# Threshold attention with an MLP: the threshold sums moved from VectorE to ScalarE, and the first loads split evenly over two queues, keys first

## The chip, the cores and the metric

The kernel runs on one core of a Trainium2 chip. The metric is the device time of one execution in microseconds (us), the median of the runs. Kernels are compared through the ratio to the unchanged kernel, run in turn with them on the same chip.

## The reference

Eight batches of eight heads with 576 tokens and head size 64, then an MLP with a squared ReLU over all 4608 tokens:

```python
scores = scale * np.matmul(q, k.transpose(0, 1, 3, 2))
thresh = np.max(scores, axis=-1, keepdims=True) - tau
scores = np.where(scores >= thresh, scores, -1000000000.0)
scores = scores - np.max(scores, axis=-1, keepdims=True)
attn = np.exp(scores)
attn = attn / (np.sum(attn, axis=-1, keepdims=True) + 1e-09)
attn_out = np.matmul(attn, v)
# heads side by side: x is (4608, 512)
h = x @ w_in            # 512 x 2048
r = np.maximum(h, 0.0)
out = (r * r) @ w_out   # 2048 x 512
```

## The kernel before

A *visit* handles a pair of heads, a *step* one block of 128 queries of both heads. Each step computes scores into PSUM, takes the row maxima on VectorE, adds -8 tau to get the threshold, exponentiates on ScalarE, and then masks and sums in one VectorE pass, after which the PSUM is free for the next scores. `s` is the PSUM tile of the scores (single buffered, one per head), `st` a small SBUF tile with a column per scalar.

```python
def scores(s):
    ...                                            # matmuls into sc[u]      (L199)
    mx, thr = (st[:, j, 0:n] for j in range(2))
    for u in range(n):
        nc.vector.tensor_reduce(out=mx[:, u:u + 1], in_=sc[u][:, :, 0:HALF], axis=AX.XY, op=ALU.max)   # L204
    nc.vector.tensor_scalar(out=thr, in0=mx, scalar1=ntau8, scalar2=None, op0=ALU.add)                 # L205

def exponents(vis, i):
    nc.scalar.activation(out=bias, in_=mx, func=AF.Copy, scale=-SCALE)                                 # L213
    for u in range(len(sc)):
        nc.scalar.activation(out=w..., in_=sc[u]..., func=AF.Exp, bias=bias[:, u:u + 1], scale=SCALE)  # L215

def threshold(vis, i):
    for u in range(n):                                                                                 # L227
        nc.vector.scalar_tensor_tensor(out=wu, in0=sc[u]..., scalar=thr[:, u:u + 1], in1=wu,
                                       op0=ALU.is_ge, op1=ALU.mult, accum_out=sm[:, u:u + 1])
    nc.vector.tensor_scalar(out=den, in0=sm, scalar1=S * LITTLE, scalar2=None, op0=ALU.max)            # L229
    nc.vector.reciprocal(rcp, den)

def prep(n):                                       # 32x32 blocks of queries and keys turned on VectorE (L178)
    for to, rows in zip((qT, kT), rows_of(n)):
        nc.vector.transpose(to, rows.rearrange("p c d -> p (c d)"))
```

In the order of VectorE's queue, L204 and L205 of a step are followed either by `prep` of the next visit (two transposes), or by three instructions that round a piece of the MLP's weights (L137, L138, L140), or by neither; then comes L227. GpSimd divides (L239), squares (L378) and does the last two steps of the rounding (L142, L144). TensorE runs one fixed queue: scores (L199), transposes of the weights of attention (L257), mixing with v (L318), and pieces of the MLP (L367 and the products L398, L430) spread between.

## Time and profile before

| | before |
|---|---|
| median of the runs ahead of the prediction | 1455.95 us |
| span of the profiled execution | 1448.2 us |
| TensorE, VectorE, ScalarE, GpSimd busy | 96, 62, 29, 43% |
| first score matmul | 8.97 us |
| threshold sums L205 on VectorE, busy | 57.4 us in 160 |

The lines that the argument rests on are in the prediction. One more of the page is of use later: the matmul clock that was granted, in tenths, in 40 slices of 36 us each. A trace's clock records know full and half speed only; the halved stretches are 3.4 or 6.8 us long here, so a slice that shows 8 held several us of half clock. The records don't start with the program: the first one of this trace is at 25.8 us, and what comes before it is counted as full speed.

```profile
PEclk9899999999999999999999999999999999999999
```

### The profile page before, as it was taken

The page shows a single profiled execution, that of the slowest core. Times are in us where ns is not written, and L with a number is a line of the kernel's source. Part 1 is how long each engine was busy: PE and PEld are TensorE (multiplying, and loading weights), DVE is VectorE, ACT ScalarE, POOL GpSimd, SP SyncE. Part 2 cuts the span into 40 slices and gives each one's busy share as a digit, 9 for nine tenths or more (in the row PEclk, how much of TensorE's full clock was granted, in tenths as well). Part 3 has the DMA queues.
Part 4 walks back from the last instruction along what each step waited for, and adds up shares of the span by engine and source line. Part 5 has one row for each costly group of instructions (what it writes and reads, how often), then busy time and mean ns, then how long its engine had stood idle before and what let it go on. Part 6 is the DMA issues. An engine that isn't in the chain of part 4 may idle for free.

```text
span 1448.2 us, 22131 instructions
## 1 busy us (share of the span) xinstructions
PE 1387.1 (96%) x7412; PEld 1058.0 (73%) x7412; DVE 904.5 (62%) x1930; ACT 423.1 (29%) x904; POOL 623.9 (43%) x794
## 2 busy tenths in 40 slices
PE   5898888999999999999999999999999999999998
PEld 3676555747787777777777777777777777788887
DVE  5899886568766676666675767666667666631011
ACT  3666554223222322222322222222222222210100
POOL 3588765425343444343343435343434352422321
PEclk9899999999999999999999999999999999999999
DMA  7564442345445545545455454555554445440000
GB/s 149 119 140 109 112 112 52 55 84 96 85 96 91 109 85 96 88 92 88 97 96 105 84 96 85 95 89 100 95 101 84 89 90 91 90 81 19 5 15 15
DMA packets 532528, 125.94 MB, mean 87 GB/s; under 512 B 523712, under 2 KB 523712, under 8 KB 532416
## 3 DMA queue, kind: packets, MB, share of 16 engines
q1 hardware_dynamic: 529984, 124.24, 44.7%
q8 instruction: 60, 0.98, 0.3%
q10 hardware_dynamic: 2400, 0.30, 0.2%
q14 instruction: 52, 0.43, 0.1%
q0 software_dynamic: 32, 0.00, 0.0%
HBM read 48.63 MB, written 9.44 MB: 40 GB/s over the span
## 4 chain that ended last, share of the span: by engine, by line
PE 65%; SPq 20%; DVE 6%; issue 3%; DMA 2%; ACT 2%; POOL 1%; DVEq 0%; ACTq 0%; POOLq 0%
PE bank L367 26%; PE bank L430 16%; SPq L299 12%; PE s L199 9%; PE bank L318 8%; SPq L306 5%; PE bank L398 3%; SPq L161 3%; DVE st L204 2%; PE bank L257 1%; SPq L163 1%; DVE w L227 1%; DVE turned L288 1%; DMA vs<-in_v_dram 1%; DVE turned L138 1%
## 5 line engine op out<-in xcount | busy, mean ns | idle before, releaser
L367 PE MATMUL bank<-xT,w_in_sb 128*128 128x256 f32 x2304 | 519.8, 382 | 3.5 <-POOL w_in_sb L144 2.4
L367 PEld LDWEIGHTS bank<-xT,w_in_sb 128*128 128x128 f32 x2304 | 431.6, 190 | 84.2 <-issue 21.3
L204 DVE TENSOR_REDUCE st<-s 128x1 f32<-128x576 f32 x288 | 206.7, 753 | 296.9 <-PE s L199 296.9
L378 POOL TENSOR_TENSOR g<-g 128x512 f32<-128x512 f32 x144 | 149.8, 1042 | 232.2 <-ACT g L377 209.4
L239 POOL TENSOR_SCALAR w<-w,st 128x576 f32<-128x576 f32 x269 | 236.4, 888 | 31.2 <-DVE st L230 25.2
L227 DVE SCALAR_TENSOR_TENSOR w<-s,st,w 128x576 f32<-128x576 f32 x269 | 207.3, 803 | 52.2 <-ACT w L215 51.9
L430 PE MATMUL bank<-wo,gsum 128*128 128x256 f32 x1024 | 234.2, 382 | 2.9 <-DVE u_sum L445 1.6
L430 PEld LDWEIGHTS bank<-wo,gsum 128*128 128x128 f32 x1024 | 192.5, 190 | 38.6 <-issue 7.6
L199 PE MATMUL s<-kT,qT 64*128 64x288 f32 x1024 | 176.8, 438 | 30.4 <-DVE kT L178 10.3
L237 POOL TENSOR_SCALAR st<-st 128x2 f32<-128x2 f32 (+1 forms) x160 | 38.7, 242 | 379.7 <-DVE w L227 366.1
L215 ACT ACTIVATE w<-s,st 128x576 f32<-128x576 f32 x269 | 186.1, 738 | 12.1 <-ACT st L213 0.4
L318 PE MATMUL bank<-wT,vs 128*64 128x128 f32 (+3 forms) x1700 | 179.7, 358 | 8.7 <-DMA wT<-turned 3.5
L430 PE MATMUL bank<-wo,g 128*128 128x256 f32 x768 | 178.7, 383 | 2.9 <-DVE osb L449 2.9
L199 PEld LDWEIGHTS s<-kT,qT 64*128 64x128 f32 x1024 | 101.1, 190 | 95.2 <-issue 71.4
L288 DVE STREAM_TRANSPOSE turned<-w 128x576 f32<-128x576 f32 x225 | 163.0, 758 | 10.1 <-DMA wT<-turned 3.8
L430 PEld LDWEIGHTS bank<-wo,g 128*128 128x128 f32 x768 | 143.8, 190 | 32.4 <-issue 8.2
L318 PEld LDWEIGHTS bank<-wT,vs 128*64 128x64 f32 x1700 | 107.9, 141 | 78.1 <-issue 25.6
L377 ACT ACTIVATE g<-bank 128x512 f32<-128x512 f32 x144 | 86.3, 599 | 200.7 <-PE bank L367 200.7
L213 ACT ACTIVATE st<-st 128x2 f32<-128x2 f32 (+1 forms) x160 | 33.2, 208 | 328.2 <-DVE st L204 327.5
L332 ACT COPY xT<-bank 128x256 f32<-128x256 f32 x42 | 15.7, 373 | 287.9 <-PE bank L318 287.9
L443 DVE TENSOR_TENSOR gsum<-g 128x512 f32<-128x512 f32 x32 | 20.8, 681 | 107.3 <-PE bank L430 107.3
L398 PE MATMUL bank<-wo,g 128*128 128x512 f32 x128 | 62.0, 619 | 7.3 <-POOL wo L144 7.0
(66 smaller groups left out, 858.1 us busy)
## 6 DMA issues: line engine op xcount, KB each, us to landing
wT<-turned SPq DMA_DIRECT2D x800, 72.0 KB, 2.2
ql<-in_q_dram SPq DMA_DIRECT2D x128, 72.0 KB, 2.5
vs<-in_v_dram SPq DMA_DIRECT2D x72, 128.0 KB, 2.5
wo<-in_moe_w_in_dram SPq DMA_DIRECT2D x16, 512.0 KB, 4.5
wo<-in_moe_w_out_dram SPq DMA_DIRECT2D x16, 512.0 KB, 3.6
out_dram<-osb SPq DMA_DIRECT2D x32, 256.0 KB, 2.3
kl<-in_k_dram SPq DMA_DIRECT2D x62, 72.0 KB, 2.6
wT<-turned SPq DMA_DIRECT2D x200, 20.0 KB, 1.9
```

The lines of the kernel that those rows point to most:

```text
L199: nc.tensor.matmul(sc[u][:, half, 0:HALF], lhsT, kT[rows, half * HALF:(half + 1) * HALF], start=True, stop=True)
L204: nc.vector.tensor_reduce(out=mx[:, u:u + 1], in_=sc[u][:, :, 0:HALF], axis=AX.XY, op=ALU.max)
L215: nc.scalar.activation(out=w[:, u, :].rearrange("p (h k) -> p h k", h=2), in_=sc[u][:, :, 0:HALF], func=AF.Exp, bias=bias[:, u:u + 1], sca ...
L227: nc.vector.scalar_tensor_tensor(out=wu, in0=sc[u][:, :, 0:HALF], scalar=thr[:, u:u + 1], in1=wu, op0=ALU.is_ge, op1=ALU.mult, accum_out=s ...
L239: nc.gpsimd.tensor_scalar(out=w[:, u, :], in0=w[:, u, :], scalar1=z[:, u:u + 1], scalar2=rcp[:, u:u + 1], op0=ALU.add, op1=ALU.mult)
L288: nc.vector.transpose(wb[:, u * KB:(u + 1) * KB, i % 2, :], w[:, u, :].rearrange("p (k q) -> p k q", q=32))
L299: nc.sync.dma_start(out=to[:, :, at:at + 64], in_=wb[rows, j::4, :, :].rearrange("p c u q -> p c (u q)"))
L318: nc.tensor.matmul(ps[u * D:(u + 1) * D, 0:nq], vs[n % 2][:, u * (NBLK + 1) + c, :], wT[:, cw, cols], start=(c == 0), stop=(c == NBLK))
L367: nc.tensor.matmul(h[:, x % 2, :], w_in_sb[:, c, f * P:(f + 1) * P], xT[:, c, at:at + TCH], start=(c == 0), stop=(c == NMC - 1))
L378: nc.gpsimd.tensor_tensor(out=to, in0=to, in1=to, op=ALU.mult)
L398: nc.tensor.matmul(o[t].rearrange("p (h d) -> p h d", h=2), g[:, f, t * P:(t + 1) * P], mov, start=(f == 0), stop=(f == NFT - 1))
L430: nc.tensor.matmul(to, left[:, f, :], wo[:, slot, f, :], start=(f == 0), stop=(f == HF - 1))
```

## The change

It is meant to shorten VectorE's queue and to have the first visit's data in SBUF sooner.

```diff
 def load_qk(n):
-        for x, t in zip(rows_of(n), (q, k)):
-            queue = nc.scalar if n == 0 and t is k else nc.sync
+        for x, t in list(zip(rows_of(n), (q, k)))[::-1]:
             for m in range(4):
+                queue = nc.scalar if n == 0 and m % 2 else nc.sync
 def scores(s):
-        mx, thr = (st[:, j, 0:n] for j in range(2))
+        mx = st[:, 0, 0:n]
         ...
-        nc.vector.tensor_scalar(out=thr, in0=mx, scalar1=ntau8, scalar2=None, op0=ALU.add)
 def exponents(vis, i):
-        mx, bias = (st[:, j, 0:len(sc)] for j in (0, 2))
+        mx, thr, bias = (st[:, j, 0:len(sc)] for j in range(3))
         nc.scalar.activation(out=bias, in_=mx, func=AF.Copy, scale=-SCALE)
+        nc.scalar.activation(out=thr, in_=mx, func=AF.Identity, bias=ntau8)
```

## The prediction

> **What bounds the kernel now.** I read the busy shares first, then a table of six stretches of time, then the matmul engine's waits, then the rows of the instructions that the change touches, and last the timeline of single steps. (A "step" is one block of 128 queries of one pair of heads.) The busy shares:
>
> ```profile
> PE 1387.1 (96%) x7412; PEld 1058.0 (73%) x7412; DVE 904.5 (62%) x1930; ACT 423.1 (29%) x904; POOL 623.9 (43%) x794
> ```
>
> TensorE is the bound over the whole, VectorE is at 62% and ScalarE at 29%, so the change moves work from a half loaded engine to a lightly loaded one, and neither is the bound. Whether there is a gain depends on the stage. Columns: stretch, its length, then busy us (number of instructions) of PE, PEld, DVE, ACT, POOL, then clock, DMA share and GB/s:
>
> ```profile
> 0.00:9.00 9.00, 0.03 (x2) 0.04 (x2) 1.71 (x3) 1.28 (x1) 2.83 (x10) 1.00 0.87 109
> 9.00:82.00 73.00, 56.80 (x369) 41.59 (x370) 59.34 (x131) 40.64 (x89) 35.21 (x48) 0.88 0.61 132
> 82.00:250.00 168.00, 149.14 (x1073) 99.40 (x1074) 142.58 (x292) 99.03 (x220) 124.52 (x139) 0.98 0.43 106
> 250.00:300.00 50.00, 50.00 (x273) 34.78 (x268) 26.76 (x59) 15.39 (x33) 18.97 (x27) 1.00 0.36 65
> 300.00:1320.00 1020.00, 1006.49 (x5123) 774.30 (x5122) 658.11 (x1416) 256.02 (x542) 415.67 (x547) 1.00 0.50 91
> 1320.00:1448.20 128.20, 124.59 (x584) 107.92 (x582) 15.98 (x32) 10.78 (x20) 26.71 (x24) 1.00 0.03 13
> ```
>
> From 250 us to the end TensorE is busy 1181.1 of 1198.2 us: 17 us idle, in which nothing on VectorE or ScalarE can save more than a few. Before 250 us it is busy 206.0 of 250: 9 us of first loads, 16 us idle between 9 and 82, 19 us idle between 82 and 250. As TensorE runs its queue in a fixed order and is dense later, a microsecond saved here comes off the end. The waits of TensorE say on what:
>
> ```profile
> PE s L199 <- DVE w L227: 11.8, 9, 3.5
> PE s L199 <- DVE kT L178: 10.3, 4, 9.0
> PE s L199 <- DVE wo L227: 9.7, 5, 3.3
> PE bank L398 <- POOL wo L144: 7.0, 5, 2.6
> ```
>
> The scores (L199) wait 21.5 us in 14 steps for the threshold pass L227, which frees their PSUM, and once 9.0 us for the first transposed keys. So the early chain is: scores, row maximum L204, threshold sum L205, other VectorE work of the step, L227, next scores. The change takes L205 out of it.
>
> **What the Trainium skill says.** (1) "SBUF — State Buffer", section "Who interferes with whom": a VectorE tensor_scalar may enter a two-port mode, and then it and GpSimd exclude each other for a whole instruction. The trace agrees: L205 on 128x2 lasts 228 ns in the median but 1327 at most, and here it ends with a GpSimd instruction:
>
> ```profile
> 55.39 1.31 DVE L205 TENSOR_SCALAR st<-st,ntau 128x2 f32<-128x2 f32 x1
> 55.40 1.27 POOL L144 TENSOR_TENSOR w_in_sb<-turned 128x512 f32<-128x512 f32 x1
> 55.82 0.22 ACT L213 ACTIVATE st<-st 128x2 f32<-128x2 f32 x1
> 56.13 1.37 ACT L215 ACTIVATE wo<-s,st 128x576 f32<-128x576 f32 x2
> 56.61 0.77 DVE L178 STREAM_TRANSPOSE qT<-ql 128x576 f32<-128x576 f32 x1
> 57.31 0.73 DVE L178 STREAM_TRANSPOSE kT<-kl 128x576 f32<-128x576 f32 x1
> 57.97 0.77 DVE L227 SCALAR_TENSOR_TENSOR wo<-s,st,wo 128x576 f32<-128x576 f32 x1
> ```
>
> (2) "ScalarE: Activation LUTs", section "What ACT_TABLE_LOAD costs": an ACTIVATE with immediate operands costs 186 ns plus 0.833 ns an element, each pointer operand adds about 93, back-to-back ones overlap by about 93; cheap functions such as Identity are in every table set. The trace has 208 ns for L213, the immediate form on two elements, against 188 by the page. (3) "DMA: Bandwidth & Descriptors", section "Issuing engines are not separate DMA queues": two issuing queues share the same engines and save only issue time. The trace shows those engines 87% busy in the first 9 us. (4) "TensorE: Matmul & The Clock Gate", Part 1, says idle windows of about 3.4 us halve the matmul clock. Here the eight score matmuls take 3.00 us at 14.73 and 21.03 us and 1.24 at 632.40: agreed.
>
> **The change, part by part.** The rows:
>
> ```profile
> L205 DVE TENSOR_SCALAR st<-st,ntau 128x2 f32<-128x2 f32 x128 | 50.6, 396 | 4.5
> L205 DVE TENSOR_SCALAR st<-st,ntau 128x1 f32<-128x1 f32 x32 | 6.8, 214 | 1.1
> L213 ACT ACTIVATE st<-st 128x2 f32<-128x2 f32 x128 | 26.6, 208 | 239.6 <-DVE st L204 238.9
> ```
>
> Removed from VectorE: 50.6 + 6.8 = 57.4 us of busy time. Only 160 x about 0.22 = 35 us of it is work; some 22 us is waiting for GpSimd. As instructions overlap, a free L205 really pushes the next instruction back by 0.13 to 0.2 us (12 steps of the timeline read this way).
>
> Added on ScalarE: 160 x (208 + 93 = 301 ns, estimate from the row and the page) = 48 us of busy time, ScalarE to about 471 us or 32%. It stands between the bias and the exponentials. The exponential now starts about 0.04 us after the bias ends; with the threshold between and the overlap, I estimate 0.15 to 0.2 us later. No second table load appears in the compiled program.
>
> So in each early step either VectorE gates L227 (gain) or the exponential does (loss of about 0.2). Going through the twelve steps up to 82 us: step 0 is gated by ScalarE (VectorE sat idle 0.78 us before L227): -0.15. Step 1, transposes between: +0.18. Step 2, ScalarE gates: -0.2. Step 3: VectorE and ScalarE ready together, and TensorE goes on late for other reasons: 0. Step 4: +0.13. Step 5 (L205 blocked for 1.31 us before the transposes): L227 can come 0.37 earlier, then ScalarE gates, and TensorE has other work until 0.2 us before: +0.2. Step 6: +0.05. Step 7, the one shown above: transposes can start at 55.4, and end at 56.8; the exponential would end near 57.05; L227 moves from 57.97 to 57.05, and TensorE sat idle 1.81 us for it: +0.9. Step 8: 0, TensorE-bound. Step 9: L205 waited 0.2 for GpSimd, but the next instruction (L137, weight rounding, also a tensor_scalar) will wait in its place: +0.1. Steps 10 and 11: +0.13 and +0.1. Sum: 1.44 us.
>
> 82 to 250 us: 24 steps, of which TensorE's waits show only a few gated by L227; there the blocked L205 is mostly followed by weight rounding, which inherits the wait. The rounded weights come a little sooner to L398. I put 0.8 us (about 6 steps of 0.13). After 250 us: 0.1.
>
> First loads: ten DMAs for the first visit, before as four on one queue and six on the other, now five and five. The compiled listing shows that the DMAs rotate over eight semaphores, so that the ninth and tenth wait for early ones to land; in the trace these were key loads issued at 3.97 and 4.95 us, and the last key landed at 8.13. Now the two late ones are query loads, on both queues at about 4.0: landing near 7.2. But VectorE still transposes queries first (7.03 to 7.8 before, while the keys were coming in) and keys second. Now both transposes must follow the last landing: 7.2 + 1.5 = 8.7 against 8.13 + 0.78 = 8.91. Gain 0.15 to 0.2, not 0.9: loading keys first works against the order of the transposes. I take 0.15.
>
> Sum: 0.15 + 1.44 + 0.8 + 0.1 = 2.5 us.
>
> **Rivals.** (a) ScalarE becomes the gate: L227 waits 51.9 us in 44 places for the exponential already. If the addition costs its full 0.3 us in every gated early step, and the gains do not show, about +3 us: 1459. Against it: ScalarE is 29% busy, and past 250 us TensorE has other matmuls to run meanwhile. (b) The clock: if step 7 shrinks, TensorE's idle gap before the scores at 58.90 halves, and these (2.69 us, warm 1.24) and the mixing matmuls after them (2.40 us, warm 1.31) may run warm. That would add 1 to 2 us to the gain: 1451.5. I count 0.6 for it. (c) The wait just moves: GpSimd excludes the next tensor_scalar instead of L205 everywhere, and the gain is the first loads and steps 5 and 7 only: 1454.7. (d) The first loads turn out worse, if one late query load lands at 8 us: start at 9.5, +0.6 us. The second visit's keys and queries come in swapped order too, but are needed only at 18.7 us.
>
> **Range and chances.** 1455.95 - 2.5 - 0.6 = 1452.8 us. The three runs before spread over 2.7 us, so a noise of 1.3 either way; with the rivals 1448.5 to 1456.8. Two per cent would be 29 us, more than all of TensorE's idle time between 9 and 82 us: faster 0.01, same 0.98, slower 0.01.
>
> **What would show it.** First score matmul at 8.6 to 8.9 us instead of 8.97. TensorE waiting under 1.2 us instead of 1.81 for the L227 of step 7. VectorE busy down by 35 to 57 us, or less where L137 and L138 inherit blocking: their means (437 and 880 ns) would rise. A new ScalarE row near 0.3 us a piece, its busy time up 40 to 50. PE idle before 82 us down by 1 to 3 us, and PE from 300 us on unchanged. I am wrong if the exponential's wait on the early steps grows so that TensorE idles longer before 82 us, if the matmul total after 300 us changes by more than 3 us, or if the first scores start after 9.2.

## The result, and the profile after

| | before | after |
|---|---|---|
| median, same chip, four runs each | 1456.62 us | 1444.49 us |
| ratio, 95% interval | | 0.9916 [0.9899, 0.9933] |
| once more on another chip, 11 and 6 runs | 1452.02 us | 1439.97 us, ratio 0.9926 [0.9911, 0.9942] |

A ratio is the mean time of one kernel's runs over that of the other's of the same rounds, so not quite the ratio of the medians. The change saves 11 to 12 us (0.0084 x 1456.6 = 12.2, and 0.0074 x 1452.0 = 10.7). The prediction said 1452.8 us and 1448.5 to 1456.8: within 2%, as forecast, but outside the range, and the gain more than three times the 3.1 us foretold (2.5 for the change and 0.6 for the clock).

The busy shares after, to be held against those of before: VectorE lost 50.4 us of busy time, ScalarE gained 12.6.

```profile
PE 1384.3 (96%) x7412; PEld 1057.4 (73%) x7412; DVE 854.1 (59%) x1770; ACT 435.7 (30%) x1064; POOL 620.9 (43%) x794
...
PEclk9999999999999999999999999999999999999999
```

ScalarE's small rise surprises only until one looks at the group itself. The sums take 36.6 + 9.0 = 45.6 us, but they overlap the bias ahead of them and the exponential after them, and busy time counts overlapping time once. The rows of the new instruction (it is L213 of the changed kernel; the bias, L213 before, has become L212) and of two others that stayed on VectorE (busy us, mean ns, then the idle time before them):

```profile
L213 ACT ACTIVATE st<-st,ntau 128x2 f32<-128x2 f32 x128 | 36.6, 286 | 0.0
...
L213 ACT ACTIVATE st<-st,ntau 128x1 f32<-128x1 f32 x32 | 9.0, 282 | 0.0
```
```profile
L137 DVE TENSOR_SCALAR turned<-wo 128x512 uint32<-128x512 uint32 x32 | 19.4, 605 | 0.0
...
L229 DVE TENSOR_SCALAR st<-st 128x2 f32<-128x2 f32 x128 | 38.8, 303 | 4.4
```

L137 had a mean of 437 ns before and L229 265: part of the blocking by GpSimd that L205 suffered was handed to the next tensor_scalar, as predicted. It is 5.4 us at L137 (19.4 against 14.0) and 4.8 at L229 (38.8 against 34.0), some 10 of the 22 us.

Now the step that the prediction shows (step 7), in the timeline after. Columns: start, duration, engine, line, operation.

```profile
52.86 0.77 DVE L178 STREAM_TRANSPOSE qT<-ql 128x576 f32<-128x576 f32 x1
52.98 1.28 POOL L144 TENSOR_TENSOR w_in_sb<-turned 128x512 f32<-128x512 f32 x1
...
53.51 0.29 ACT L213 ACTIVATE st<-st,ntau 128x2 f32<-128x2 f32 x1
53.55 0.73 DVE L178 STREAM_TRANSPOSE kT<-kl 128x576 f32<-128x576 f32 x1
...
54.49 0.82 DVE L227 SCALAR_TENSOR_TENSOR wo<-s,st,wo 128x576 f32<-128x576 f32 x1 [0.21 <-ACT wo L215]
...
55.47 0.72 PE L199 MATMUL s<-kT,qT 64*128 64x288 f32 x2 [0.80 <-DVE wo L227]
```

The same GpSimd instruction runs, but no VectorE instruction stands behind it: the transposes go on beside it. TensorE waits 0.80 us where it waited 1.81, and L227 now waits a little for the exponential. That much is the mechanism of the prediction. What does not fit is the size, and one thing more: the stretch of 9 to 82 us shows TensorE *busy* for as long as before.

```profile
9.00:82.00 73.00, 57.38 (x405) 41.71 (x403) 60.58 (x128) 44.06 (x108) 40.43 (x53) 1.00 0.68 144
300.00:1320.00 1020.00, 1006.64 (x5133) 777.17 (x5132) 616.59 (x1295) 265.69 (x658) 411.86 (x544) 1.00 0.50 91
```

Before it was 56.80 us there, for 369 matmuls; now 57.38 us, for 405. A window of fixed ends hides a gain that shifts work into it. The Trainium skill, "Trainium Kernel Development and Optimization", section "Performance Expectations", calls matmul busy time a bad metric for how close a kernel is to its limit, because matmuls are pipelined. It is no measure of progress in these traces either: nearly equal busy time, a tenth more matmuls. A reason that the traces show is the clock, 0.88 in this stretch before and 1.00 after: at half clock a matmul is busy for longer.

So a better ruler was needed. Both programs issue the same 7412 matmuls in the same order. I numbered them and subtracted the start of each in one trace from that of the same matmul in the other. The growth of this lead between two matmuls is the time saved between them. The marks are the first matmul, the one at 82 us in the kernel before (number 369) and the one at 250 us (number 1441).

| stretch of the program | foretold | traces before (three) | traces after (three) | saved, means |
|---|---|---|---|---|
| to the first scores | 0.15 | 8.97, 8.81, 8.48 | 8.47, 8.42, 7.83 | see below |
| first scores to 82 us | 1.44 (and 0.6 for the clock) | 73.07, 73.66, 73.96 | 68.19, 68.17, 68.29 | 5.3 |
| 82 to 250 us | 0.8 | 168.02, 169.36, 168.44 | 168.20, 165.68, 167.24 | 1.6 |
| 250 us to near the end | 0.1 | 1190.05, 1191.28, 1191.49 | 1189.48, 1187.96, 1191.64 | 1.2 |

The traces before are those of the kernel before (twice) and of the one with only its loads changed; those after are of the changed kernel (twice) and of the one that also transposes keys first. The first stretch is sharp: 73 to 74 against 68.2. The later ones scatter by as much as they differ. All together the three traces before are 8.7 us longer than the three after; the timed runs differ by 10.7 to 12.2 us, so the traces account for most of the gain and not for all of it.

By the records the clock was halved for 17 to 20 us of the first 82 in every one of the three traces before, and in none of the three after (the trace of the thresholds alone, w2 below, had 10 us of it and took 71.40 us there). These numbers leave out the start: the records begin at 25 to 26 us in the traces before and at 32 to 33 us in those after, and until then the score matmuls are slow in both (3.00 us for the eight of steps 1 and 2, where w13 and w14 have 1.94). What a halved stretch does is to be seen at step 8, first before (half clock from 60.0 to 66.8 us), then after:

```profile
62.98 2.40 PE L318 MATMUL bank<-wT,vs 128*64 128x128 f32 x20
...
66.15 1.08 PE L199 MATMUL s<-kT,qT 64*128 64x288 f32 x4
```
```profile
58.15 1.31 PE L318 MATMUL bank<-wT,vs 128*64 128x128 f32 x20
...
60.73 1.46 PE L199 MATMUL s<-kT,qT 64*128 64x288 f32 x6 [0.80 <-DVE w L227]
```

Before, TensorE's own slow matmuls fill the step (its scores take 2.69 us, the mixing 2.40), 7.26 us, and the next scores wait for nobody; after (1.94 and 1.31), the step takes 5.27 us and they wait 0.80 us for L227. So the first question was whether the clock or the chain made the gain (theories C and L in the expectations).

### The profile page after: what moved, and what is told of

Its sections match the earlier page's. It is cut to its first block, busy times and chain, and to the rows that moved or that the text cites. A ratio compares the mean times of both kernels' runs of the same rounds, so it can differ in the third digit from the quotient of the medians.

```text
span 1442.4 us, 21966 instructions
## 1 busy us (share of the span) xinstructions
PE 1384.3 (96%) x7412; PEld 1057.4 (73%) x7412; DVE 854.1 (59%) x1770; ACT 435.7 (30%) x1064; POOL 620.9 (43%) x794
## 4 chain that ended last, share of the span: by engine, by line
PE 61%; SPq 23%; DVE 8%; issue 3%; DMA 3%; ACT 1%; POOL 1%; DVEq 0%; ACTq 0%; POOLq 0%
PE bank L367 25%; PE bank L430 16%; SPq L299 13%; PE s L199 9%; PE bank L318 7%; SPq L306 5%; PE bank L398 3%; SPq L161 3%; DVE st L204 1%; DVE w L227 1%; DMA wT<-turned 1%; DVE turned L288 1%; DVE turned L138 1%; PE bank L257 1%; DVE turned L137 1%
## 5 line engine op out<-in xcount | busy, mean ns | idle before, releaser
L227 DVE SCALAR_TENSOR_TENSOR w<-s,st,w 128x576 f32<-128x576 f32 x269 | 207.6, 805 | 80.6 <-ACT w L215 80.4
L430 PE MATMUL bank<-wo,gsum 128*128 128x256 f32 x1024 | 234.0, 381 | 1.4 <-DVE u_sum L445 1.4
L430 PEld LDWEIGHTS bank<-wo,gsum 128*128 128x128 f32 x1024 | 192.6, 190 | 36.4 <-issue 7.2
L199 PE MATMUL s<-kT,qT 64*128 64x288 f32 x1024 | 176.5, 440 | 27.4 <-DVE w L227 10.7
L318 PE MATMUL bank<-wT,vs 128*64 128x128 f32 (+3 forms) x1700 | 179.4, 357 | 11.5 <-DMA wT<-turned 4.7
L430 PE MATMUL bank<-wo,g 128*128 128x256 f32 x768 | 178.7, 383 | 2.1 <-DVE osb L449 2.1
L199 PEld LDWEIGHTS s<-kT,qT 64*128 64x128 f32 x1024 | 100.6, 191 | 91.1 <-issue 64.2
L318 PEld LDWEIGHTS bank<-wT,vs 128*64 128x64 f32 x1700 | 107.6, 139 | 81.3 <-issue 29.9
L430 PEld LDWEIGHTS bank<-wo,g 128*128 128x128 f32 x768 | 143.8, 190 | 31.6 <-issue 8.2
L212 ACT ACTIVATE st<-st 128x2 f32<-128x2 f32 (+1 forms) x160 | 33.3, 208 | 325.6 <-DVE st L204 324.8
```

What stands on the lines that cost most here:

```text
L199: nc.tensor.matmul(sc[u][:, half, 0:HALF], lhsT, kT[rows, half * HALF:(half + 1) * HALF], start=True, stop=True)
L227: nc.vector.scalar_tensor_tensor(out=wu, in0=sc[u][:, :, 0:HALF], scalar=thr[:, u:u + 1], in1=wu, op0=ALU.is_ge, op1=ALU.mult, accum_out=s ...
L318: nc.tensor.matmul(ps[u * D:(u + 1) * D, 0:nq], vs[n % 2][:, u * (NBLK + 1) + c, :], wT[:, cw, cols], start=(c == 0), stop=(c == NBLK))
L430: nc.tensor.matmul(to, left[:, f, :], wo[:, slot, f, :], start=(f == 0), stop=(f == HF - 1))
```

## The experiments

Each was timed in five rounds beside the kernel before. From the mean granted clock of a run its half-clock time can be had: (1 - clock) x 2 x span. It is the half-clock time of the records, so it leaves out the start, too.

**The parts, and both kernels again (w1 to w4).** Copies of both kernels, the changed one with the old loads (w2), and the kernel before with the new loads (w3). The diffs are the two halves of the change.

> The unchanged kernel as an entry of its own, so that the span and the mean granted clock of each of its timed runs are recorded. Theory C (the matmul clock dropping to half in the idle gaps of the first 80 us is most of the gain): timed runs near 1456 us have a lower mean clock than the profiled 0.992, about 0.989 to 0.990 (24 us of half clock there; about 5 to 8 us more), and the slower a run, the lower its clock. Theory L (the freed VectorE chain alone, at a fixed clock): the clock is 0.992 in all of them and does not follow the time.

> Thresholds on ScalarE, first loads as before. If the thresholds carry the gain (theory C or L): 1444 to 1446 us, 10 to 12 us under the kernel before, first scores at 8.97 us. If the first loads carry it through the phase of the clock window (theory F): 1452 to 1455 us.

> First loads split and keys first, thresholds on VectorE as before. Theories C and L: first scores at 8.5 us and 0.5 to 1 us under the kernel before. Theory F: 5 to 10 us under it, at a mean clock near 0.994.

> The whole change once more, beside the parts on the same chip: 1443 to 1445 us, clock 0.993 to 0.996. If the parts simply add, its gain is the sum of the gains of the two parts within 1.5 us.

| run | median us | ratio to before | mean half-clock time |
|---|---|---|---|
| w1 before again | 1452.97 | 1.0008 [0.9994, 1.0022] | 28 us |
| w2 thresholds only | 1443.11 | 0.9931 [0.9915, 0.9948] | 18 us |
| w3 loads only | 1452.24 | 1.0002 [0.9987, 1.0017] | 31 us |
| w4 after again | 1439.97 | 0.9926 [0.9911, 0.9942] | 16 us |

The thresholds carry the gain; the loads alone give nothing that these intervals could show. They do move the first scores from 8.81 to 8.48 us, but with a spread of 5 us between runs 0.4 us is not to be seen in the time. Theory F is out. The two parts together make 9.7 us (10.0 and -0.3), the whole change 10.7 on the same chip, so they add within the 1.5 us expected.

The clock does follow the time within a kernel: over all runs of the kernel before and of w1 to w12 (102) a microsecond of half clock costs 0.20 us, standard error 0.03. The 11 us or so that the changed kernel runs less at half clock are then worth 0.20 x 11 = 2.2 us, a fifth of the gain, not most of it. This is a correlation, and over recorded half clock only, so the next runs change the clock on purpose.

**Clock kept up by filling (w5, w6).** Transposes of the identity into an unused quarter of a PSUM bank, in the gaps in which TensorE waits during the first steps.

```diff
+    def warm(count):
+        for _ in range(count):
+            nc.tensor.transpose(bank[7][:, 3 * P:4 * P], ident, ident)
+    FILL = {0: 24, 1: 18, 2: 18}
     for s in range(END + 1):
         state["step"] = s
+        if early():
+            warm(FILL.get(s, 5))
```

> The kernel before, with transposes of the identity matrix into an unused quarter of a PSUM bank put where TensorE waits in the first steps, so that its clock is not halved there. Theory C (most of the gain is the clock of the first 80 us): no half-clock stretch before 80 us, and the time falls by 6 us or more under the kernel before. Theory L (mostly the VectorE chain): it falls by at most what the faster first score matmuls give, 2 to 4 us, and the changed kernel still leads it by 6 us or more.

> The changed kernel with the same filling. Theory C: the gap between this and the filled kernel before shrinks to 3 to 4 us, since the clock no longer differs. Theory L: the gap stays at 8 to 11 us. In both the first steps get shorter than in the unfilled changed kernel (scores 1.24 us instead of 3.00), so 2 to 5 us under it.

w5: 1449.02 us, ratio 0.9965 [0.9945, 0.9984]. w6: 1436.88 us, ratio 0.9880 [0.9865, 0.9894]. The gap between the filled kernels is 0.85% or 12.4 us, no smaller than unfilled (an estimate from the two intervals: give or take 3.5). That speaks for L. But the filling itself was worth 5.1 us in the kernel before, more than the 2 to 4 of theory L and less than the 6 of theory C, and in the trace of w5 it had not done its whole work: 13.7 us of half clock were left in the first stretch (6.8 in that of w6).

**Blocking without the move (w7).** The sum stays on VectorE, but by columns. No 128x1 sum was ever blocked in the trace before.

```diff
-        nc.vector.tensor_scalar(out=thr, in0=mx, scalar1=ntau8, scalar2=None, op0=ALU.add)
+        for u in range(n):
+            nc.vector.tensor_scalar(out=thr[:, u:u + 1], in0=mx[:, u:u + 1], scalar1=ntau8, scalar2=None, op0=ALU.add)
```

> Threshold sums still on VectorE, but as two sums of 128x1 where there was one of 128x2; all 128x1 sums of before lasted 214 ns, none blocked by GpSimd. If blocking by GpSimd (about 22 us of L205's 57) is what the change removed from the chain: 4 us or more under the kernel before. If it is the mere presence of the instruction on VectorE: equal to the kernel before within 2 us, or slower. If blocking only moves to the next tensor_scalar: mean of L137 rises from 437 ns, time within 2 us of before.

1449.97 us, ratio 0.9973 [0.9960, 0.9987]: 3.9 us faster than before, just short of the 4 expected, though VectorE now has 288 sums in place of 160. Their mean is 208 ns: none blocked. L137 rose from 437 to 627 ns, so blocking is handed on where a rounding follows. In its trace the stretch to 82 us took 69.20 us, against 73 to 74 before and 68.2 after. Steps 5 and 7, whose sum was blocked, are 1.0 us shorter each (5.26 us); step 8 is 1.9 us shorter, but this trace records no half clock before 82 us, so that part may be the clock's. The blocking alone is thus worth about 2 us there, and perhaps more. After 250 us taking it away brings nothing (1192.70 us).

**Keys transposed first (w8).** `prep(0)` turns the keys ahead of the queries.

> The changed kernel, and in the first visit VectorE transposes the keys before the queries. If the late transposes of the queries hold the start back as predicted: first scores at about 7.8 us instead of 8.47, and 0.5 to 1 us under the changed kernel, if the later clock windows do not hide it.

The first scores came at 7.83 us instead of 8.42 to 8.47, as expected: in the changed kernel both transposes wait for the last query to land (6.98 us), and then follow each other. The time: 1440.99 us, ratio 0.9910 [0.9892, 0.9928], not distinguishable from the changed kernel's 0.9926 and 0.9916. A saving of 0.6 us cannot be told from nothing here.

**What the sum costs on ScalarE (w9, w10).** Once issued twice, once taken out altogether, with the maximum used as the threshold; the latter gives a wrong result.

```diff
# w9
         nc.scalar.activation(out=thr, in_=mx, func=AF.Identity, bias=ntau8)
+        nc.scalar.activation(out=st[:, 7, 0:len(sc)], in_=mx, func=AF.Identity, bias=ntau8)
# w10
-        nc.scalar.activation(out=thr, in_=mx, func=AF.Identity, bias=ntau8)
-        thr, sm, den, rcp = (st[:, j, 0:n] for j in (1, 3, 4, 5))
+        thr, sm, den, rcp = (st[:, j, 0:n] for j in (0, 3, 4, 5))
```

> The changed kernel with the threshold activation issued twice on ScalarE, the second result unused: it doubles the only cost that the change adds. If the sum is nearly free on ScalarE (theory L, bias to exponential 0.29 us instead of 0.24): within 1.5 us of the changed kernel, that is 10 to 12 us under the kernel before. If each costs the 0.15 to 0.2 us of the prediction on the chain: 2 to 4 us slower than the changed kernel.

> Wrong on purpose: no threshold sum on any engine, the row maximum itself is compared with. It shows what a free sum would be worth. Theory L with a nearly free ScalarE: within 1.5 us of the changed kernel. If ScalarE's part still costs: 3 us or more under it.

w9: 1445.64 us, ratio 0.9951 [0.9938, 0.9963], so 3 to 5 us slower than the changed kernel: my expectation of a nearly free sum failed for the second one. w10: 1441.01 us, ratio 0.9917 [0.9900, 0.9933], where the changed kernel has 0.9926 and 0.9916: the first one is free within the noise. The two go together once the timelines are read, here of step 0, first of the changed kernel and then of w9:

```profile
12.25 0.20 ACT L212 ACTIVATE st<-st 128x2 f32<-128x2 f32 x1 [6.88 <-DVE st L204]
12.36 0.28 ACT L213 ACTIVATE st<-st,ntau 128x2 f32<-128x2 f32 x1
12.54 1.35 ACT L215 ACTIVATE w<-s,st 128x576 f32<-128x576 f32 x2
```
```profile
12.19 0.20 ACT L212 ACTIVATE st<-st 128x2 f32<-128x2 f32 x1 [6.63 <-DVE st L204]
12.30 0.28 ACT L213 ACTIVATE st<-st,ntau 128x2 f32<-128x2 f32 x1
12.49 0.28 ACT L214 ACTIVATE st<-st,ntau 128x2 f32<-128x2 f32 x1
12.68 1.35 ACT L216 ACTIVATE w<-s,st 128x576 f32<-128x576 f32 x2
```

The exponential needs the bias, and starts 285 ns after it in the median of all steps in the kernel before. With one sum between, it starts after 296 ns; with two, after 480. The first sum fits into a gap that the exponential would have waited out anyway and costs 11 ns; the second has no gap left and costs 184.

**Filling and keys first (w11), mixing later (w12).** w11 joins w6 and w8. In w12 the mixing matmuls of the later visits come one step later in TensorE's queue (`mixed = {1: (0, 5), NBLK: (2, 5)}` instead of 4 and 4).

> The changed kernel with the filling of the first waits and with the keys transposed first: if both keep their gains, 0.6 us under the filled changed kernel, that is 17 to 18 us under the kernel before.

> The changed kernel, with the mixing matmuls of the later visits (L318) one step later in TensorE's order. After 250 us the traces show the changed kernel gaining 3.0 us at the scores and 2.8 at the products and giving back 2 to 5 us at L318, which waits for the rearranging DMAs. If that give-back is a deadline missed by those DMAs: L318's waits for DMA fall from 12.6 us to under 5 and the time is 3 to 5 us under the changed kernel. If the DMAs are simply slower or other waits take their place: same within 1.5 us.

w11: 1436.87 us, ratio 0.9889 [0.9870, 0.9907], no different from w6. w12: 1444.49 us, ratio 0.9941 [0.9922, 0.9960], if anything slower than the changed kernel. To see why w12 was tried: matched matmul by matmul after 250 us, for two traces before against two after, the products L430 gain 2.7 to 2.9 us and the scores L199 3.0 to 3.1, while the mixing L318 gives back 2.4 to 5.4. Some of TensorE's waits before, after, and in w12 after 250 us (total us, times, longest):

```profile
PE bank L318 <- DMA wT<-turned: 3.5, 4, 1.7
PE bank L430 <- DVE osb L449: 2.9, 2, 1.9
```
```profile
PE bank L318 <- DMA wT<-turned: 4.7, 5, 2.4
...
PE bank L430 <- DVE osb L449: 2.1, 2, 1.4
```
```profile
PE bank L430 <- DVE osb L449: 3.8, 4, 2.0
PE s L199 <- DVE w L227: 3.1, 4, 1.7
```

The products wait for VectorE to empty their banks, and VectorE gets there sooner without L205 in its queue; the mixing waits for the DMAs that rearrange the weights of attention, and TensorE, coming sooner, meets them earlier. That last link is read from the traces and not tested by itself. In w12 that wait of the matmuls is gone (1.5 us of it are left at TensorE's weight loads), but waits for VectorE have come in its place, so moving the mixing is no cure. (The 12.6 us of the expectation is in none of these lists.) Nor does the give-back always come: in the filled pair w13 and w14 below, the scores gain 3.1 us, the products 2.2, and the mixing gives back nothing.

**The clock settled (w13, w14).** Still open was the early stretch, as no trace had the old sums there at full clock. The filling was raised to eight transposes a gap and 36 ahead of the first scores.

> The kernel before with eight filling transposes in each early wait instead of five (36 ahead of the first scores). Wanted: a trace of VectorE's thresholds without any half clock before 82 us. If the chain itself carries the early gain: 3 to 4.5 us longer up to the 370th matmul of the program (82 us in the kernel before) than the changed kernel filled alike, with 6.2 to 6.3 us in the two or three steps whose sum is blocked. If the clock carries it: at most 2 us longer.

> The changed kernel filled alike: steps of 5.2 to 5.3 us, no half clock before 82 us; the gap in time to the filled kernel before 10 to 12 us if the chain carries it, 6 to 8 if a third of the whole gain was the clock.

w13: 1447.20 us, ratio 0.9964 [0.9946, 0.9983], mean half-clock time 19 us. w14: 1437.29 us, ratio 0.9891 [0.9871, 0.9912], 17 us. With nearly the same half-clock time the gap is 1 - 0.9891 / 0.9964 = 0.73%, or 10.6 us (estimated from the intervals: give or take 4): the whole gain of the unfilled kernels on the same measure (10.7 and 12.2). w5 and w6 gave 12.4, so nothing is seen of a part that goes with the clock, though a part of 2 us could hide in the noise. In their traces, w13 has one stretch of half clock before 82 us (at 21.1 us, 3.4 long), w14 none, and the stretch to matmul 369 takes 67.17 against 62.73 us: 4.4 us from the chain, of which the one halved stretch, in step 2, can have made 0.3 at most. The lengths of the steps, from first scores to first scores:

| step | 0 | 1 | 2 | 3 | 4 | 5 | 6 | 7 | 8 | 9 | 10 | 11 | sum |
|---|---|---|---|---|---|---|---|---|---|---|---|---|---|
| w13 | 4.71 | 5.24 | 5.54 | 6.19 | 5.47 | 6.27 | 5.48 | 6.27 | 5.48 | 6.54 | 4.54 | 6.32 | 68.05 |
| w14 | 4.75 | 4.94 | 5.24 | 5.28 | 5.26 | 5.26 | 5.56 | 5.27 | 5.26 | 6.10 | 4.38 | 6.13 | 63.43 |
| saved | -0.04 | 0.30 | 0.30 | 0.91 | 0.21 | 1.01 | -0.08 | 1.00 | 0.22 | 0.44 | 0.16 | 0.19 | 4.62 |
| saved without filling | -0.04 | 0.31 | -0.05 | 0.13 | 0.61 | 1.01 | -0.10 | 1.01 | 2.11 | -0.20 | 0.55 | 0.08 | 5.42 |
| foretold | -0.15 | 0.18 | -0.20 | 0 | 0.13 | 0.20 | 0.05 | 0.90 | 0 | 0.10 | 0.13 | 0.10 | 1.44 |

The row "saved without filling" is the change as it was made: means of the three traces before less those of the three after. It has nearly the same sum in other places. In steps 2 and 3 TensorE is slow in both kernels, and next to nothing is saved. In steps 4, 8 and 10 half clock was recorded in at least two of the three traces before and in none after, and they save 3.3 us where the filled pair saves 0.6.

Step 5 at full clock, first in w13 and then in w14 (from its scores to the next):

```profile
36.02 1.94 PE L199 MATMUL s<-kT,qT 64*128 64x288 f32 x8
...
38.80 1.30 DVE L205 TENSOR_SCALAR st<-st,ntau 128x2 f32<-128x2 f32 x1
38.80 1.27 POOL L144 TENSOR_TENSOR w_in_sb<-turned 128x512 f32<-128x512 f32 x1
...
42.29 0.96 PE L199 MATMUL s<-kT,qT 64*128 64x288 f32 x3 [0.93 <-DVE w L227]
```
```profile
34.17 1.93 PE L199 MATMUL s<-kT,qT 64*128 64x288 f32 x8
...
36.94 1.28 POOL L144 TENSOR_TENSOR w_in_sb<-turned 128x512 f32<-128x512 f32 x1
...
39.43 0.75 PE L199 MATMUL s<-kT,qT 64*128 64x288 f32 x2
```

The sum and GpSimd's last rounding step become ready within a few nanoseconds of each other; presumably both hang on the step's rhythm, for it is the same kind of step that is blocked again and again (3, 5, 7 and 9, for 1.2 to 1.3 us each in w13). Those four steps make 3.36 of the 4.62 us.

The best versions measured are the filled changed kernels w6, w11 and w14, at ratios of 0.9880 to 0.9891 to the kernel before, 4 to 7 us under the change as made (0.9916 to 0.9926). They cannot be told apart.

## Why the prediction was wrong, point by point

**The step that failed** is "Going through the twelve steps up to 82 us", with its sum of 1.44 us; the stretch saved 5.3. The mechanism was right: the sum leaves the chain from the row maximum to the masking pass, the blocking by GpSimd leaves with it where transposes follow, and the rounding inherits it where a rounding follows. Terms of the sum were mis-sized, for three reasons that the runs show.

1. *Step 5 was read from a stretch in which the clock was halved.* I gave it 0.2, as TensorE seemed to have other work until shortly before. That other work was the mixing and the transposes at half clock: the mixing took 2.35 us there and 1.31 at full clock. Step 5 saved 1.01 us, what step 7 saved, with filling and without. For step 3 my 0 held only because TensorE was slow there in both kernels (0.13 saved); at full clock it is 0.91.

2. *Step 8 was given 0 as "TensorE-bound".* It was bound by TensorE at half clock, and saved 2.11 us without filling and 0.22 with it. Rival (b) named this very step, with 1 to 2 us, and I counted 0.6 us for it. Whether the change drove off the half clock there or whether the halved stretches fell otherwise by themselves, three traces a side can't tell.

3. *ScalarE's cost was put at 0.15 to 0.2 us a step, and charged to every step where the exponential gates.* It is 11 ns a step, since the sum falls into the time in which the exponential waits for its bias (w9, w10). The -0.15 and -0.20 of steps 0 and 2 came out as -0.04 and -0.05 (step 2, with TensorE slow; 0.30 in the filled pair). The figure itself is not wrong: it is what a second sum costs.

The early stretch, with the clock's 0.6, is 3.3 us of what the prediction missed; the rest lies later, or in the difference between traces and timed runs.

**After 250 us** I put 0.1 us, as TensorE was busy 1181.1 of 1198.2 us there. The filled pair w13 and w14 differs by 5.6 us in that stretch (1193.58 and 1187.94), the unfilled traces by 1.2 on average, and matched line by line the scores and products gain nearly 6 us before the mixing gives back a part (5.3 in the filled pair, with nothing given back). "Nothing can save more than a few" roughly held as a bound, and 0.1 was the wrong size. The traces scatter too much to give it better than 1 to 6 us. w7, which leaves the sums on VectorE unblocked, gains nothing there in its one trace, which speaks for VectorE's time and not the blocking as the source of this part. Between 82 and 250 us the unfilled traces give 1.6 us on average and the filled pair 0.4, against 0.8 foretold; that stays unsettled.

**The first loads.** Foretold as nearly worthless because the transposes keep their order; the loads alone indeed gave 1.0002. The first scores came at 8.47 us, just ahead of the foretold 8.6 to 8.9, and w8 shows the reason given to be right: with the keys transposed first it is 7.83.

**The rivals.** (a) ScalarE as the gate: no loss seen. L227 does wait longer for the exponential, 80.4 us in place of 51.9 in the main group, step 7 included; but w10, without any sum, is no faster. Its 1459 us lay outside the stated range, which should have included it. (b) The clock: recorded half-clock time did fall, from some 27 to 16 us a run, and the correlation makes that 2 us; step 8 is where the traces show it. Its sizes were off: the scores of that step take 1.94 us at full clock, not the 1.24 of a later step. Nor does the trace agree with the idle windows of about 3.4 us that the prediction quotes: its slow scores at 14.73 and 21.03 us lie before the first clock record, and the recorded halvings came after shorter idle times (last section). Filled alike, the kernels differ by no less, as far as the intervals of about 4 us tell, so the clock's part is not on top of the chain's. That a shorter chain keeps the clock up, because TensorE idles less, is likely but not shown. (c) The wait moves on: about half of the blocking does. (d) was wrong.

**What was to be seen.** VectorE's busy time fell by 50.4 us (35 to 57 foretold), the new row is 286 ns (301 foretold), L137 and L138 rose, TensorE's wait in step 7 fell to 0.80 us (under 1.2 foretold). ScalarE's busy time rose by 12.6 us, not 40 to 50, since the sums overlap their neighbours.

## What to carry to other kernels

Before a wait is sized from a trace, see at what clock the engine ran that seemed to have other work meanwhile: at half clock it hides the wait that will gate next. See also where the clock records begin. A tiny instruction costs most where it can be blocked by another engine and least where its queue is waiting for a result anyway; so look for the gap between an instruction and the one that needs its output, and fit one, not two, in there. When two programs issue the same matmuls in the same order, match them one by one; windows with fixed ends and busy shares hid a gain of 5 us here.

## What the Trainium skill lacked or had wrong

- "ScalarE: Activation LUTs", section "What ACT_TABLE_LOAD costs", is right on the cost of the sum, with its one pointer operand: 186 + 93 + 1.7 = 281 ns, and the trace has a median of 281. For the immediate form it is low: 186 + 1.7 = 188 ns against a median of 204 (L213 before). It lacks that an activation whose bias was written by the one just before starts only 285 ns after that one's start, and that a small activation between them then costs 11 ns, a second 184.
- "SBUF — State Buffer", section "Who interferes with whom", is borne out by L205's 1.3 us beside GpSimd's L144. The one-element form was never blocked: 288 sums of 128x1 had a mean of 208 ns, and the kernel was 0.27% faster than with 160 of mostly 128x2. The section leaves the conditions of the mode to another page, so this is no gap in the skill. What it doesn't say is that the block passes to the next tensor_scalar in the queue, here L137 from 437 to 605 ns.
- "TensorE: Matmul & The Clock Gate", Part 1, puts the ramp at under 1% of a span. The runs agree and give a price: 0.20 us (standard error 0.03) for each us at recorded half clock (a correlation), 3 to 38 us of which were recorded in a run, differing from run to run of one kernel. Its idle window of about 3.4 us is longer than what was enough here: in the traces of the kernel before and of the changed kernel, the longest idle time of TensorE in the 6.8 us ahead of each of nine recorded halvings was 1.6 to 2.4 us. No page says that filling the gaps with idle transposes pays: 0.35% here before the change, 0.3 to 0.5% after.
